# A convolution and gated MLP on one core: the convolution's steps in a new order, its transfers on two queues by name

## The chip, the cores and the metric

The kernel runs on one core of a Trainium2 chip. The core has five engines that run side by side, each in the order of its own instructions: TensorE (PE, with its weight loads shown as PEld), VectorE (DVE), ScalarE (ACT), GpSimd (POOL) and SyncE (SP). Transfers are issued by SP, POOL or ScalarE and carried out by 16 DMA engines. The metric is the device time of one execution in microseconds; less is better. Where the text says clock, it is the share of TensorE's full clock that the profile shows as granted.

## The reference

Two residual blocks on a sequence of 2048 tokens with 576 channels, both modulated by a vector `c`:

```python
mod = (_silu(c) @ w_mod).reshape(c.shape[0], 6, 1, -1)
h = _layernorm(x) * (1 + ca) + sa
x = x + ga * A(h)          # a long convolution, with u * Dskip
h = _layernorm(x) * (1 + cb) + sb
x = x + gb * B(h)          # a gated MLP that mixes tokens
```

`A` builds for each of 576 channels a kernel of length 2048 from 128 complex poles, `K[d, l] = Re(sum_n C P^l dB)` with `P = exp(dt * A)`, and convolves it with the sequence (in the reference by an FFT of length 4096). `B` is `z = gelu(h @ w_in)`, split in `z1` and a layer-normed `z2` (2304 columns each), `g = w_sp @ z2 + b_sp` over the 2048 tokens, and `(z1 * g) @ w_out`.

## The kernel before

The program has three parts one after the other: the convolution (`ssm`), the first half of the MLP (`phase_a`: layer norm, `z2`, and the splitting of weights into two halves of 16 bit) and its second half (`phase_b`: token mixing, gate and output). The change is in the first alone, up to the point where the first block of tokens is transposed for `phase_a`.

The convolution is written as some 50 kinds of small steps, functions under the decorator `step`, and a list, `ORDER` (line 172), of 1172 words such as `u_p.1.3`: a kind and its indices. A loop goes through the list and calls one function per word. The instructions are kept in program order on each engine, so the list fixes what each engine does after what; between engines the program waits by semaphores. An engine whose next instruction lacks its data stands still, also where later ones could run; the same holds for a queue of transfers.

The steps, in the order in which data goes through them:

- `pole_in`, `pl.0.k`, `pl.1.k`, `pload`: load the poles (set 0 is the first quarter, set 1 the rest), prepare phases and logarithms in 24 small stages on VectorE and ScalarE, store them split in three 16-bit parts, load them back in another layout.
- `load`, `mod_init`, `m_l`, `m_p`, `m_a`, `m_q`, `m_e`: constants and the modulation vectors.
- `x_l`, `st_a`, `st_v`, `ln_r`, `ln_p`, `ln_a`: the layer norm of 16 token blocks, its transform on TensorE, and the store of the result to memory (`u1_d`). `turn` ends this: all of `u1_d` is stored, and its buffers are given to the convolution.
- For each of 36 groups of 16 channels: `e_p`, `e_a` (exponentials), `t_p`, `t_i`, `t_b`, `s_f`, `s_c` (phases rounded to a period, sines), `p_a`, `p_b`, `p_c` (their products on VectorE), `kg_p`, `kg_a`, `kg_d` (the kernel, with Dskip), `k1_p`, `k1_e` (its transform). `MODE` gives for each group how the phase is rounded: 0 with a ScalarE pass and two VectorE passes; 1 to 4 with the rounding done by additional matmuls (12 instead of 4), and then a VectorE copy and a VectorE pass (1), one VectorE pass (2), a ScalarE copy and a VectorE pass (3) or one ScalarE pass (4). `COPY` says whether `k1_e` runs on VectorE ("1") or ScalarE ("0").
- For each of five channel blocks `c` (four of 128 channels, one of 64) and its parts `i`: `u_l` (load from `u1_d`), `u_p`, `u_a` (with two transfers that swap the halves of a tile), `z_p`, `z_m` (multiply with the kernel's transform), `v_p`, `v_a` (with the store to `v_d`).
- For each block and quarter `q`: `y_v` (load of `v_d`, once all its parts are stored), `y_x` (load of the residual), `y_p`, `y_s` (add, and store to `x1_d`).
- `wpre`, `ml.*`: steps of the MLP taken into the list: the loads of `w_in` for `z2` (`start_load`), their sums, scales and splitting, the first token block's layer norm. `end` gives back the memory of the tables; `ml.start` (line 1104) sets up the MLP's tiles in it and loads `ident`, `mrow`, `x1l` and `xz`, four transfers on SP.

Queues: the function `Q` puts a load on POOL's queue where its word stands in `GPQ` (line 167), else on SP's. Only loads go through `Q`. The stores of `ln_a`, `v_a` and `y_s`, the swaps of `u_a` and the loads of `pload` are on POOL; `st4_l`, `wpre`, `ml.start`, `ml.start_x1` and `ml.start_load` are on SP.

Of the kernel before, what the change touches and what calls it, by code (L numbers as in the profile page):

```python
# [18 lines left out]
D = 576  # L19
# [8 lines left out]
CHL = CHW[-1]  # L28
# [161 lines left out]
k1_p.5 kg_a.6 t_p.9 k1_e.5 u_l.0.5 kg_d.6 t_i.9 s_c.8 u_l.0.3 k1_e.4 t_p.10 t_i.10 t_b.9 s_f.9 t_b.10 s_c.9 kg_p.7 p_a.8 p_b.8 kg_a.7 kg_d.7 u_p.0.0  # L190
p_c.8 s_f.10 u_p.0.1 k1_p.6 k1_e.6 u_a.0.0 e_p.9.0 e_a.9.0 k1_p.7 e_p.11.0 u_a.0.1 kg_p.8 kg_a.8 e_a.11.0 k1_e.7 p_a.9 u_p.0.5 p_b.9 p_c.9 kg_d.8
e_p.10.0 e_a.10.0 u_p.0.3 t_p.11 u_a.0.3 t_i.11 cst_l.0 t_p.12 pload.2.0 t_i.12 z_p.0.0 s_c.10 t_b.12 u_a.0.5 u_l.0.4 kg_p.9 s_c.12 z_m.0.0 u_l.2.2
kg_a.9 s_f.12 t_b.11 s_c.11 pload.2.2 s_f.11 y_x.0.2 kg_d.9 p_a.10 z_p.0.1 z_m.0.1 p_b.10 p_c.10 v_p.0.0 u_l.1.3 k1_p.8 k1_e.8 v_a.0.0 u_p.0.2 p_a.11
cst_l.3 p_b.11 e_p.15.1 e_p.15.0 e_a.15.1 e_a.15.0 cst_l.1 t_p.14 e_p.12.1 t_i.14 e_a.12.1 u_l.1.0 z_p.0.3 kg_p.10 u_a.0.2 e_p.14.0 kg_a.10 kg_d.10
e_a.14.0 t_b.14 z_m.0.3 v_p.0.1 v_a.0.1 e_p.12.0 e_a.12.0 p_a.12 e_p.14.1 e_a.14.1 e_p.13.1 e_a.13.1 e_p.13.0 st4_l p_b.12 e_a.13.0 k1_p.10 k1_e.10
p_c.11 z_p.0.2 k1_p.9 s_c.14 u_p.0.4 u_a.0.4 t_p.13 s_f.14 t_i.13 k1_e.9 u_l.0.7 v_p.0.3 u_l.1.2 t_p.15 p_c.12 kg_p.12 v_a.0.3 t_b.13 z_m.0.2 t_i.15
p_a.14 t_b.15 kg_a.12 s_f.13 kg_d.12 kg_p.11 kg_a.11 p_b.14 p_c.14 s_c.15 v_p.0.2 t_p.16 s_f.15 z_p.0.5 z_m.0.5 v_a.0.2 s_c.13 p_a.13 p_b.13 pload.2.1
k1_p.12 t_i.16 t_b.16 s_c.16 s_f.16 kg_d.11 kg_p.14 kg_a.14 kg_d.14 u_p.1.0 u_l.1.1 u_a.1.0 u_p.1.3 u_a.1.3 p_c.13 z_p.0.4 z_m.0.4 k1_e.12 e_p.18.1
k1_p.14 k1_e.14 e_p.16.0 e_a.16.0 e_a.18.1 kg_p.13 e_p.17.1 t_p.17 p_a.15 kg_a.13 p_b.15 p_c.15 kg_d.13 e_p.17.0 e_a.17.0 u_p.0.7 t_i.17 u_l.0.6
u_p.0.6 u_a.0.6 e_p.18.0 k1_p.11 u_a.0.7 e_a.18.0 t_b.17 u_l.1.7 k1_p.13 k1_e.13 k1_e.11 e_p.16.1 e_a.16.1 t_p.18 e_a.17.1 t_i.18 t_b.18 s_c.17  # L200
v_p.0.5 v_a.0.5 u_l.1.4 p_a.16 p_b.16 s_c.18 p_c.16 s_f.18 s_f.17 v_p.0.4 v_a.0.4 e_p.19.0 e_a.19.0 z_p.0.6 z_m.0.6 kg_p.15 kg_a.15 e_p.20.0 kg_p.16
v_p.0.6 v_a.0.6 e_a.20.0 e_p.19.1 e_a.19.1 e_p.21.1 e_a.21.1 p_a.18 t_p.20 t_i.20 p_b.18 kg_d.15 k1_p.15 pload.3.0 z_p.0.7 e_p.20.1 t_b.20 kg_a.16
p_c.18 k1_e.15 z_m.0.7 y_x.0.0 e_a.20.1 t_p.19 z_p.1.0 z_m.1.0 t_i.19 u_p.1.2 u_p.1.7 u_p.1.1 kg_d.16 t_b.19 p_a.17 s_f.20 u_a.1.2 s_c.20 p_b.17
p_c.17 s_c.19 kg_p.18 kg_a.18 kg_d.18 v_p.1.0 v_a.1.0 s_f.19 pload.3.1 t_p.21 t_i.21 u_a.1.1 p_a.20 p_b.20 v_p.0.7 v_a.0.7 e_p.21.0 e_a.21.0 z_p.1.3
z_m.1.3 e_p.22.0 u_a.1.7 k1_p.16 k1_e.16 wpre.0 kg_p.17 kg_a.17 e_p.23.1 p_c.20 k1_p.18 kg_d.17 e_a.22.0 e_a.23.1 z_p.1.1 e_p.22.1 t_p.22 k1_e.18
p_a.19 p_b.19 k1_p.17 e_a.22.1 t_i.22 t_b.21 z_m.1.1 e_p.23.0 e_a.23.0 p_c.19 t_b.22 s_c.21 u_l.1.6 kg_p.20 z_p.1.2 kg_a.20 t_p.23 t_i.23 t_b.23
s_f.21 v_p.1.3 v_a.1.3 s_f.23 s_c.23 k1_e.17 kg_p.19 kg_a.19 u_p.1.6 u_a.1.6 z_m.1.2 kg_d.20 k1_p.20 k1_e.20 u_p.1.4 u_a.1.4 p_a.21 p_b.21 p_c.21
kg_d.19 p_a.23 p_b.23 t_p.24 t_i.24 t_b.24 v_p.1.2 v_a.1.2 kg_p.21 s_f.22 k1_p.19 k1_e.19 u_l.2.3 kg_a.21 kg_d.21 s_c.22 s_c.24 pload.3.2 p_a.22
p_b.22 e_p.27.0 v_p.1.1 v_a.1.1 u_p.2.3 u_a.2.3 k1_p.21 s_f.24 y_v.0.0 z_p.1.7 k1_e.21 p_c.22 z_m.1.7 y_p.0.0 e_p.27.1 e_a.27.1 wpre.1 p_c.23 e_p.24.0
e_a.24.0 y_s.0.0 kg_p.22 kg_a.22 kg_d.22 e_p.24.1 z_p.1.4 e_a.27.0 z_m.1.4 u_l.2.0 t_p.26 t_i.26 e_a.24.1 t_b.26 kg_p.23 kg_a.23 y_v.0.1 kg_d.23  # L210
e_p.26.0 e_a.26.0 v_p.1.4 e_p.25.0 e_p.25.1 e_a.25.1 u_l.1.5 u_p.1.5 v_a.1.4 p_a.24 p_b.24 p_c.24 e_a.25.0 u_a.1.5 u_l.2.6 k1_p.23 k1_e.23 t_p.27
k1_p.22 t_i.27 t_b.27 y_x.0.1 e_p.28.0 e_a.28.0 y_p.0.1 y_s.0.1 e_p.26.1 e_a.26.1 k1_e.22 z_p.1.6 t_p.25 t_i.25 z_p.1.5 s_c.26 u_p.2.2 z_m.1.5 t_b.25
t_p.30 kg_p.24 kg_a.24 s_f.26 u_l.2.4 p_a.26 u_a.2.2 p_b.26 v_p.1.7 v_a.1.7 v_p.1.5 s_f.25 v_a.1.5 e_p.32.0 p_c.26 s_c.25 y_v.0.2 z_m.1.6 u_p.2.0
u_a.2.0 s_c.27 p_a.25 y_p.0.2 y_s.0.2 u_p.2.4 u_l.2.1 u_l.2.5 kg_p.26 s_f.27 kg_a.26 y_x.1.3 z_p.2.2 z_m.2.2 kg_d.26 p_b.25 e_a.32.0 p_c.25 v_p.1.6
v_a.1.6 t_i.30 u_a.2.4 z_p.2.0 z_m.2.0 k1_p.26 t_b.30 k1_e.26 t_p.28 y_v.0.3 t_i.28 v_p.2.2 kg_d.24 e_p.28.1 e_a.28.1 u_p.2.1 v_a.2.2 u_a.2.1 e_p.30.1
# [23 lines left out]
def ssm(tc, I, x1_d, consts_s, dram, mod_d, mlp):  # L239
    nc = mlp.tied  # L240
# [4 lines left out]
    with ExitStack() as ctx:  # L245
# [174 lines left out]
        def pload(c, n):  # L420
# [5 lines left out]
            for h in range(2):  # L426
                G.dma_start(t_[64 * h:64 * h + 48], d_[c, h, k:k + 6].rearrange("q (c g n) -> (q c) g n", c=8, g=9))
# [1933 lines left out]
```

## Time and profile before

| what | us |
|---|---|
| time, median of 3 runs | 1761.44 (1759.05 to 1761.78) |
| the profiled execution's own time | 1761.1 |
| its span in the profile | 1759.3 |
| busy in the span: PE, DVE, ACT, POOL | 1661.2, 1253.8, 832.4, 275.0 |
| the first transpose of `phase_a` (the list's end) | at 428.05 |
| the first matmul of `phase_b` | 682.74 |

The profile shows one execution; times in it count from its start. An engine's busy time is the union of its instructions' spans; the ends of matmuls are modelled, so a busy PE need not be PE at its peak. In rows of the timeline stand start, duration, engine, line, operation, what it writes and reads, the number of instructions merged, and in brackets the idle time of the engine before the first of them and what ended it. Nearly all rows name line 152, that of the helper which records the instructions; tiles tell them apart: `u<-u_d` is `u_l`, `u<-v_d` is `y_v`, `pk<-u,small` is `u_p`, `pk<-small,kab` is `k1_p`, `pk<-u,st` is `y_p`, `u_d<-st1o` the store of `ln_a`, `wst` the weights of `start_load`, `pg<-et,ft` is `p_a` or `p_b`.

### The profile page before, as it was taken

What the parts mean: (1) busy time and instruction counts of PE and PEld (TensorE: products, weight loads), DVE (VectorE), ACT (ScalarE), POOL (GpSimd) and SP (SyncE); (2) the same over time, 40 slices, a digit from 0 to 9 for tenths busy, and PEclk for the clock granted to TensorE, in tenths of its full rate; (3) what the DMA queues carried; (4) which work ended last, traced back from release to release, by engine and by line L of the source; (5) the groups of instructions that cost most, each with busy time, mean ns of one, the idle gap of its engine ahead of it and who ended that gap; (6) DMA issues with size and microseconds to landing.
All of it is one profiled execution on the core that took longest, in us unless ns stands there. A gap on an engine that the chain in (4) does not pass through costs nothing. (4 is left out here: it accounts for less than half of the span.)

```text
span 1759.3 us, 36489 instructions
## 1 busy us (share of the span) xinstructions
PE 1661.2 (94%) x15246; PEld 1240.5 (71%) x15246; DVE 1253.8 (71%) x2254; ACT 832.4 (47%) x1107; POOL 275.0 (16%) x442
## 2 busy tenths in 40 slices
PE   4687999987999999999999999999999999999999
PEld 1244666655455445778878888888888888888887
DVE  5887888857989996788998777787343487334432
ACT  4868999853676664455443443333222223122210
POOL 3343334333122210000000000000111100111100
PEclk9678999998999999999999999999999999999999
DMA  8566656788598888677665877674766563556531
GB/s 237 175 194 204 182 153 185 209 234 270 187 297 259 236 246 270 246 258 280 213 203 184 315 266 269 233 241 138 243 228 233 190 217 104 204 201 208 192 109 42
DMA packets 167061, 376.25 MB, mean 214 GB/s; under 512 B 36288, under 2 KB 85056, under 8 KB 166128
## 3 DMA queue, kind: packets, MB, share of 16 engines
q0 software_dynamic: 40176, 183.48, 31.6%
q1 hardware_dynamic: 120816, 163.77, 30.7%
q10 hardware_dynamic: 5904, 26.67, 3.7%
q8 instruction: 120, 1.97, 0.5%
q14 instruction: 45, 0.37, 0.1%
HBM read 263.11 MB, written 101.31 MB: 207 GB/s over the span
## 5 line engine op out<-in xcount | busy, mean ns | idle before, releaser
L152 PEld LDWEIGHTS <-zset 128*128 128x128 f16 x7182 | 701.8, 98 | 93.5 <-DVE zset L152 8.5
L152 PE MATMUL ps<-wsp,zset 128*128 128x256 f16 x6048 | 667.7, 273 | 8.0 <-DVE zset L152 6.5
L152 PE MATMUL pz<-wz,nt 128*128 128x512 f16 (+1 forms) x1120 | 222.1, 358 | 10.8 <-DVE nt L152 4.3
L152 ACT ACTIVATE z<-gt 128x1024 f16<-128x1024 f32 x56 | 59.0, 1054 | 289.4 <-DVE gt L152 289.4
L152 PEld LDWEIGHTS <-nt 128*128 128x128 f16 x1120 | 109.0, 98 | 117.7 <-DVE nt L152 5.7
L2069 POOL DMA_DIRECT2D zset<-set_d x96 | 50.8, 529 | 870.0 <-PE ps L152 627.8
L152 DVE SCALAR_TENSOR_TENSOR gt<-ps,sc,bsp 128x512 f32<-128x512 f32 x36 | 27.0, 750 | 205.2 <-PE ps L152 203.4
L152 PE MATMUL ps<-wout,z 128*128 128x288 f16 x1344 | 170.0, 286 | 0.0
L152 PEld LDWEIGHTS <-z 128*128 128x128 f16 x1344 | 131.5, 98 | 33.0
L152 PE MATMUL ps<-n2o,zset 128*128 128x256 f16 x1134 | 128.2, 273 | 0.0
L152 DVE TENSOR_TENSOR raw<-raw 128x512 f32<-128x512 f32 (+2 forms) x228 | 119.1, 528 | 12.3 <-DMA raw<-z_d 7.8
L152 DVE SCALAR_TENSOR_TENSOR gt<-ps,sc,gt 128x512 f32<-128x512 f32 (+1 forms) x180 | 122.2, 696 | 7.6
L152 DVE TENSOR_TENSOR zset<-raw,zset 128x1792 f16<-128x1792 f32 x48 | 96.9, 2019 | 16.2 <-ACT zset L152 16.1
L152 ACT ACTIVATE zset<-raw 128x1792 f16<-128x1792 f32 x48 | 81.0, 1691 | 56.7 <-PE ps L152 20.6
L152 DVE TENSOR_TENSOR z<-ps,z 128x512 f32<-128x512 f32 (+1 forms) x126 | 71.9, 598 | 36.8 <-ACT z L152 25.0
L152 DVE TENSOR_TENSOR pg<-et,ft 128x1024 f32<-128x1024 f32 x72 | 85.5, 1218 | 3.3 <-PE pk L152 2.0
L152 PE MATMUL pk<-zz,small 128*128 128x512 f32 x144 | 70.1, 613 | 0.0
L152 ACT ACTIVATE wsp<-raw,sc 128x1792 f16<-128x1792 f32 x25 | 44.6, 1785 | 42.7 <-DVE raw L152 35.0
L152 ACT ACTIVATE z<-z,sc 128x1024 f32<-128x1024 f32 x21 | 24.1, 1148 | 75.6 <-DVE z L152 71.9
L152 DVE TENSOR_TENSOR zz<-pk,uu 128x1024 f32<-128x1024 f32 x36 | 44.0, 1221 | 19.8 <-PE pk L152 18.9
L152 ACT ACTIVATE z<-pz,sc 128x512 f32<-128x512 f32 (+1 forms) x96 | 51.5, 582 | 13.5 <-DMA z_d<-z 11.8
L152 ACT ACTIVATE z<-z,nm,r 128x1152 f32<-128x1152 f32 x24 | 31.5, 1342 | 54.1 <-DVE nm L152 31.6
(311 smaller groups left out, 2409.0 us busy)
## 6 DMA issues: line engine op xcount, KB each, us to landing
zset<-set_d POOLq DMA_DIRECT2D x96, 896.0 KB, 5.0
raw<-z_d SPq DMA_DIRECT2D x48, 512.0 KB, 5.7
set_d<-zset ACTq DMA_DIRECT2D x24, 896.0 KB, 6.1
z_d<-z POOLq DMA_DIRECT2D x32, 576.0 KB, 9.6
zset<-wa_d POOLq DMA_DIRECT2D x18, 896.0 KB, 4.9
raw<-in_w_spT SPq DMA_DIRECT2D x25, 512.0 KB, 4.4
set_d<-zset SPq DMA_DIRECT2D x12, 896.0 KB, 5.8
u_d<-st1o POOLq DMA_DIRECT2D x16, 576.0 KB, 3.8
```

What stands on the lines that cost most here:

```text
L152: return self.tc.keep_in_program_order(f(*a, **k))
L2069: self.nc.gpsimd.dma_start(o, self.set_d[f, j - 1] if j else self.wa_d[f])
```

## The change

- `ORDER` is another list of the same steps, with three new ones. `MODE`, `COPY` and `GPQ` are set anew with it. `MODE` has 16, 2, 6, 4 and 8 groups of modes 0 to 4 where it had 17, 3, 6, 6 and 4. `COPY` puts 22 of 36 copies on VectorE where it put 14. `GPQ` names 123 steps where it named 41.
- The stores of `ln_a`, `v_a` and `y_s`, the swaps of `u_a`, the loads of `pload`, `st4_l`, `wpre`, `start_load` and `start_x1` go through `Q` too: on SP's queue unless their word stands in `GPQ`.
- The loads of `mrow`, `x1l` and `xz` leave `ml.start` and become the steps `ml.ld_m`, `ml.ld_l` and `ml.ld_z`, placed in the list by themselves.

By the lists, SP issues 122 transfers before and 177 after, POOL 258 (memsets included) and 203.

The parts of the list that the text speaks of, before:

```
... ln_p.14.1 s_c.7 e_p.10.1 p_a.7 p_b.7 ln_a.14.1 e_a.11.1 ln_p.14.0 ln_a.14.0 turn u_l.0.2 cst_l.2 kg_p.6 p_c.7
... z_p.3.7 kg_p.34 kg_a.34 kg_d.34 k1_p.35 k1_e.35 k1_e.33 k1_p.34 end ml.start ml.ap y_x.4.1 u_p.4.1 y_x.4.0
    u_a.4.1 k1_e.34 u_p.3.4 z_m.3.7 y_v.1.2 ml.start_sum.1 v_p.3.1 v_a.3.1 z_p.3.5 u_a.3.4 v_p.3.7 v_a.3.7 z_m.3.5
    y_p.1.2 ml.start_x1 ml.win_scale.6.0
... y_s.3.1 y_s.4.1 y_v.3.2 y_p.3.2 y_s.3.2 y_v.4.2 y_p.4.2 y_x.4.2 y_s.4.2 y_v.4.3 ml.start_load.3 y_p.4.3 y_s.3.3 y_s.4.3
```

and after:

```
... ln_p.14.0 ln_a.14.0 e_p.8.1 e_a.8.1 e_p.9.1 e_a.9.1 ln_p.14.1 ln_a.14.1 turn t_p.8 t_i.8 cst_l.2 p_a.7 p_b.7 p_c.7
    e_p.8.0 e_a.8.0 p_a.6 p_b.6 p_c.6
... z_p.3.0 k1_p.35 k1_e.35 y_v.1.2 z_m.3.0 kg_d.33 y_p.1.2 kg_p.34 kg_a.34 u_a.4.2 k1_p.33 kg_d.34 k1_p.34 end
    ml.start ml.ld_z ml.start_sum.1 ml.start_load.2 ml.ld_l k1_e.33 v_p.3.0 v_a.3.0 u_p.4.0 y_s.1.2
... y_s.4.1 y_x.4.3 y_p.4.2 y_s.4.2 y_p.3.2 y_x.3.3 y_p.4.3 y_s.4.3 y_x.3.1 y_s.3.1 y_x.3.2 y_s.3.2 ml.start_load.3 y_s.3.3
```

The rest of the diff, cut to its core:

```diff
-MODE = [int(k) for k in "333301130222221440204304000000000000"]
-COPY = "010001110000011111010000000100100011"
+MODE = [int(k) for k in "332433110422204440022444000000000000"]
+COPY = "110011111110011111111100010001100100"
...
         def pload(c, n):
+            Q_ = Q("pload", c, n)
...
-                G.dma_start(t_[64 * h:64 * h + 48], d_[c, h, k:k + 6].rearrange("q (c g n) -> (q c) g n", c=8, g=9))
+                Q_.dma_start(t_[64 * h:64 * h + 48], d_[c, h, k:k + 6].rearrange("q (c g n) -> (q c) g n", c=8, g=9))
...
-            G.dma_start(u1_d[:, b:b + 2, :, :, c].rearrange("g b r k d -> (b r k) g d"), o)
+            Q("ln_a", b, h).dma_start(u1_d[:, b:b + 2, :, :, c].rearrange("g b r k d -> (b r k) g d"), o)
...
         def wpre(q):
             mlp.nc = nc
+            mlp.ldq = Q("wpre", q)
             mlp.start_load(q, pools["wpre"])
...
-            G.dma_start(uu[:64, 1], uu[64:, 0])
-            G.dma_start(uu[64:, 1], uu[:64, 0])
+            Q("u_a", c, i).dma_start(uu[:64, 1], uu[64:, 0])
+            Q("u_a", c, i).dma_start(uu[64:, 1], uu[:64, 0])
...
-            G.dma_start(v_d[c][:, kr(c, i)], by(v, c))
+            Q("v_a", c, i).dma_start(v_d[c][:, kr(c, i)], by(v, c))
...
-            G.dma_start(x1_d[bs, :, chan(c)].rearrange("b p d -> p b d"), xb)
+            Q("y_s", c, q).dma_start(x1_d[bs, :, chan(c)].rearrange("b p d -> p b d"), xb)
...
         def ml(name, *a):
-            mlp.nc = nc
+            mlp.nc, mlp.ldq = nc, Q("ml", name, *a)
...
     def win_load(self, t, c0, n):
-        S, I = self.nc.sync, self.I
+        S, I = self.ldq or self.nc.sync, self.I
...
-        S.dma_start(mrow, self.mod_d[:2].partition_broadcast(128))
...
-        S.dma_start(self.x1l, I["x"][:, 4:, D - CHL:])
...
-        S.dma_start(self.x1f[:, :, 384:], I["x"][:, :4, 384:])
         self.stg = self.pool(self.c2, "stg", 2)
 
+    def ld_m(self):
+        self.ldq.dma_start(self.mrow, self.mod_d[:2].partition_broadcast(128))
+
+    def ld_l(self):
+        self.ldq.dma_start(self.x1l, self.I["x"][:, 4:, D - CHL:])
+
+    def ld_z(self):
+        self.ldq.dma_start(self.x1f[:, :, 384:], self.I["x"][:, :4, 384:])
+
     def start_x1(self):
-        self.nc.sync.dma_start(self.x1f[:, :, :384], self.x1_d[:4, :, :384].rearrange("b p d -> p b d"))
+        self.ldq.dma_start(self.x1f[:, :, :384], self.x1_d[:4, :, :384].rearrange("b p d -> p b d"))
```

More of the change, by code (lines that the diff above doesn't have):

```diff
@@ L190 @@
[L190 to L193, printed above, removed]
@@ L206 @@
[L206 to L209, printed above, removed]
@@ L210 @@
[L210 to L213, printed above, removed]
@@ L226 @@
-p_a.35 e_p.34.0 u_p.4.2 t_b.34 e_p.34.1 u_a.3.7 u_a.4.2 p_b.35 p_c.35 e_a.34.0 e_a.34.1 y_x.2.1 u_l.4.3 v_p.3.3 v_a.3.3 kg_p.33 kg_a.33 kg_d.33
-y_p.2.0 k1_p.32 z_p.3.1 y_s.2.0 z_m.3.1 s_c.34 k1_e.32 u_l.3.5 s_f.34 p_a.34 v_p.3.0 v_a.3.0 u_l.3.4 u_p.3.5 u_a.3.5 kg_p.35 k1_p.33 y_v.2.3 p_b.34
-p_c.34 kg_a.35 kg_d.35 z_p.3.7 kg_p.34 kg_a.34 kg_d.34 k1_p.35 k1_e.35 k1_e.33 k1_p.34 end ml.start ml.ap y_x.4.1 u_p.4.1 y_x.4.0 u_a.4.1 k1_e.34
-u_p.3.4 z_m.3.7 y_v.1.2 ml.start_sum.1 v_p.3.1 v_a.3.1 z_p.3.5 u_a.3.4 v_p.3.7 v_a.3.7 z_m.3.5 y_p.1.2 ml.start_x1 ml.win_scale.6.0 v_p.3.5 v_a.3.5
```

126 lines of the change are left out of this document (73 added, 53 removed).

## The prediction

> **What bounds the kernel now.** I read the page first, then busy time by stretches, the timeline at the places where TensorE idles, the waits of the DMA queue, and the groups of instructions for durations. The page's span and engine totals, and the stretches that I cut at the changes of regime (columns: stretch, length, busy us and instructions of PE, PEld, DVE, ACT, POOL, then granted TensorE clock, DMA share, GB/s):
>
> ```profile
> span 1759.3 us, 36489 instructions
> ...
> PE 1661.2 (94%) x15246; PEld 1240.5 (71%) x15246; DVE 1253.8 (71%) x2254; ACT 832.4 (47%) x1107; POOL 275.0 (16%) x442
> ```
>
> ```profile
> 0.00:60.00 60.00, 27.36 (x121) 9.64 (x122) 40.35 (x119) 35.45 (x64) 22.30 (x40) 0.94 0.75 206
> 60.00:160.00 100.00, 73.63 (x1189) 39.97 (x1188) 83.56 (x176) 78.11 (x108) 32.58 (x49) 0.72 0.62 197
> 160.00:365.00 205.00, 204.91 (x2967) 124.58 (x2966) 178.33 (x218) 183.92 (x245) 82.33 (x136) 1.00 0.65 187
> 365.00:430.00 65.00, 50.52 (x433) 35.77 (x430) 37.00 (x91) 23.78 (x30) 25.55 (x38) 0.87 0.88 263
> 430.00:685.00 255.00, 242.29 (x1280) 125.36 (x1279) 230.55 (x692) 168.72 (x259) 51.88 (x68) 1.00 0.82 248
> ```
>
> The changed list is the convolution alone, the first 428 us; what follows keeps its code and starts when the list ends, so a microsecond won before 428 is one won at the end. Of those 428 us, 205 are TensorE without a gap: no order of steps makes them shorter, except by moving TensorE's work out of them. What an order can win lies before 160 us (no engine above 84%), where the layer norm hands over to the convolution, and after 365, where transfers set the pace (0.88 of the DMA engines).
>
> The hand-over, on POOL, SP, PE and DVE:
>
> ```profile
> 146.74 0.75 POOL L152 DMA_DIRECT2D u_d<-st1o  x1 [2.31 <-ACT st1o L152]
> ...
> 150.85 0.77 POOL L152 DMA_DIRECT2D u<-u_d  x1 [2.82 <-DVE k L152]
> ```
>
> ```profile
> 150.33 1.63 SPq L152 DMA_DIRECT2D u<-u_d  x3
> ```
>
> ```profile
> 151.83 0.29 PE L152 MATMUL pk<-et,pg 128*32 128x64 f32 x8
> 156.97 3.75 PE L152 MATMUL pk<-u,small 128*128 128x512 f32 x4 [4.84 <-DMA u<-u_d]
> 160.65 1.62 PE L152 MATMUL pk<-small,kab 128*64 128x128 f32 x16
> ```
>
> ```profile
> 162.32 0.69 DVE L152 COPY k<-pk 128x512 f32<-128x512 f32 x1 [4.01 <-PE pk L152]
> ```
>
> ```profile
> 152.00:157.00 5.00, 0.16 (x11) 0.07 (x1) 4.71 (x6) 4.92 (x7) 0.57 (x1) 0.79 0.97 281
> 157.00:162.00 5.00, 5.00 (x20) 2.46 (x20) 1.31 (x3) 1.88 (x2) 1.08 (x2) 0.52 0.47 135
> ```
>
> The last store of the layer norm (`ln_a.14.0`) is issued at 146.7, the first loads (`u_l`) at 150.3 when it has landed, and TensorE gets their data at 157.0. It has run out of other work at 152.1, waits 4.84 us, and then runs at a granted clock of 0.52.
>
> The tail: SP's queue (first its longest wait on VectorE between 160 and 430 us, then its issues), then PE and DVE:
>
> ```profile
> SPq L152 <- DVE kab L152: 12.4, 1, 12.4
> ```
>
> ```profile
> 367.98 0.33 SPq L152 DMA_DIRECT2D mrow<-mod_d  x1
> 368.36 0.44 SPq L152 DMA_DIRECT2D x1l<-in_x  x1
> 368.89 1.12 SPq L152 DMA_DIRECT2D xz<-in_x  x1
> 370.29 4.61 SPq L152 DMA_DIRECT2D u<-v_d  x1
> ```
>
> ```profile
> 381.83 0.66 PE L152 MATMUL pk<-u,st 128*64 128x128 f32 x2 [6.39 <-DMA u<-v_d]
> ```
>
> ```profile
> 385.48 0.16 DVE L152 COPY sc<-pk 128x1 f32<-128x1 f32 x1 [10.49 <-PE pk L152]
> ```
>
> `ml.start` puts the load of `mrow` on SP; its memory is that of the tables, so it waits 12.4 us for the last `kg_d`. Behind it stand `x1l`, `xz` and the loads of `y_v.1.2`, whose first takes 4.61 us to issue, and TensorE, whose next step is `y_p.1.2`, stands still for 6.39 us, VectorE for 10.49.
>
> **The change part by part.** *Engines.* Durations of what `MODE` and `COPY` move:
>
> ```profile
> L152 ACT ACT_TABLE_LOAD x37 | 47.5, 1283 | 1.4 <-PEq L2350 0.7
> ...
> L152 DVE SCALAR_TENSOR_TENSOR ft<-ft,ps 128x1024 f32<-128x1024 f32 x17 | 20.6, 1213 | 2.2 <-ACT ft L152 2.2
> ...
> L152 ACT ACTIVATE ft<-ps 128x1024 f32<-128x1024 f32 x20 | 20.6, 1029 | 2.1 <-PE ps L152 2.1
> ...
> L152 DVE TENSOR_SCALAR ft<-ft 128x1024 int32<-128x1024 int32 x26 | 18.1, 701 | 3.4 <-ACT ft L152 2.8
> ...
> L152 ACT ACTIVATE k<-pk 128x512 f32<-128x512 f32 x22 | 13.2, 602 | 1.0 <-PE pk L152 0.8
> ```
>
> Modes 0 to 4 go from 17, 3, 6, 6, 4 groups to 16, 2, 6, 4, 8. On VectorE mode 0 costs 1.21 + 0.70 us, mode 1 about the same, mode 3 0.70, mode 4 nothing: 1.9 + 1.9 + 2 x 0.7 = 5.2 us less. Eight more `k1_e` copies go to VectorE, at about the 0.69 of the copy quoted above: 5.5 us more. VectorE ends even, at +0.3. ScalarE loses the eight copies (-4.8) and gains two passes of about 1.03 net and loses one of like size (+1): 3.8 us less. TensorE gets one more group with the rounding matmuls (eight more, 0 to 1.6 us at 0.2 each; I take 0.6). These sums are small because the plan rebalances; the rest is order.
>
> *Start, 0 to 150 us.* Counting where the list goes from exponentials to sines and back reproduces the 37 table loads of the page; the new list has 36, but 12 instead of 15 before `turn`: 3 x 1.28 = 3.8 us less of ScalarE there. It idles 21.9 us between 60 and 160, so most of this may be covered; without that cover it is worth the 3.8. The first steps are also exchanged:
>
> ```profile
> 11.43 0.17 DVE L152 TENSOR_SCALAR ec<-ec 96x6 f32<-96x6 f32 x1 [5.16 <-ACT ec L152]
> ...
> 13.15 0.67 ACT L152 ACTIVATE st1o<-ln_x 128x576 f32<-128x576 f32 x1
> ```
>
> `mod_init`, behind which VectorE's pole steps queued for 5.16 us, comes far later; but `st_a.0.0`, whose VectorE part needs `x_l.0` (here at 13.15), comes far earlier, so VectorE, with some 4 us of work listed ahead of it, waits there instead: about 5 us. I put the whole stage at -1. Bounds: all table loads and the removed wait without a substitute, -9; the new wait with one further statistics step behind it, +3.
>
> *Hand-over.* In the new list `p_a` to `p_c` of groups 6 and 7 stand behind `turn` instead of mostly before:
>
> ```profile
> L152 DVE TENSOR_TENSOR pg<-et,ft 128x1024 f32<-128x1024 f32 x72 | 85.5, 1218 | 3.3 <-PE pk L152 2.0 <-ACT ft L152 1.0
> ...
> L152 DVE SCALAR_TENSOR_TENSOR et<-ft,et 128x512 f32<-128x512 f32 x36 | 24.8, 689 | 0.8
> ```
>
> That is 2 x (2 x 1.22 + 2 x 0.69) = 7.6 us of VectorE's work which now lies in the 10.2 us between the last store (146.74) and the data (156.97), so the stores can go out earlier by up to as much, and there is work while they fly. Won: the 4.84 us gap and what the low clock cost behind it, by these rows at full clock:
>
> ```profile
> 257.58 1.02 PE L152 MATMUL pk<-u,small 128*128 128x512 f32 x2
> ...
> 258.53 0.85 PEld L152 LDWEIGHTS pk<-small,kab 128*64 128x64 f32 x16 [0.76 <-issue]
> 258.54 1.09 PE L152 MATMUL pk<-small,kab 128*64 128x128 f32 x16
> ```
>
> 3.75 - 2 x 1.02 = 1.7 and 1.62 - 1.09 = 0.5, together with the gap 7.0 at most. VectorE's own gap says 4.0 at least if the data come in time. I take -6, with 0 as the other bound, should the loads still be late.
>
> *Middle.* TensorE-bound before, and I see nothing that ends that: through the middle VectorE's listed work leads TensorE's by the same in both lists (by 23.8 us before and 24.6 after at `p_c.20`, 21.8 and 20.4 at `p_c.35`, adding up the list with mean durations like those quoted). `k1_p.7` (1.0), `e_p.9.0` and `e_p.11.0` (some 0.3 each) move ahead of the first `u_p`, so 1.6 less is left there; with the 0.6 above, -1. What it may cost is the first rival.
>
> *Tail.* `y_v.1.2` now stands before `end` on SP and the loads of `mrow`, `x1l`, `xz` (`ml.ld_*`) on POOL's queue behind it, so the 6.39 us end; late next is whatever the DMA engines deliver last. They were busy 0.88 of 65 us, or 57 us, and the bytes are nearly the same, so at most 7.8 us can go. I take two thirds of that, -5; bounds -7.8 and 0.
>
> *End of the list.* A loss:
>
> ```profile
> 428.05 0.76 PE L152 MATMUL pt<-ident,n 128*128 128x128 f32 x5
> ```
>
> ```profile
> 424.05 10.11 SPq L152 DMA_DIRECT2D wst<-in_w_in  x6
> ```
>
> ```profile
> 434.01 2.34 ACT L152 ACTIVATE wz<-wst 128x2560 f16<-128x2560 f32 x1 [4.34 <-DMA wst<-in_w_in]
> ```
>
> ```profile
> uu<-in_x SPq DMA_DIRECT2D x4, 256.0 KB, 4.4
> ```
>
> Before, `ml.start_load.3` is issued 4 us ahead of the first transpose of the next phase. Now the stores `y_s.4.3`, `y_s.3.1` and `y_s.3.2` stand ahead of it on SP; `y_s.3.1` needs `y_x.3.1`, a load that stands on POOL behind `y_s.4.2` and `y_x.3.3`: two issues of 0.75 and 4.4 to landing, about 6 us after `y_s.4.2`. So the weights come later by about 5, against 1 or 2 of slack. Bounds: 0 (the DMA engines are free by then) and +6; I take +5.
>
> The sum: -1 - 6 - 1 - 5 + 5 = -8, against the profiled execution's own 1761.1 (span 1759.3 and 1.8 around it): **1753**. The median of the runs shown is 1761.44, 0.3 above it, so the same holds there.
>
> **The rivals.** *Stores before loads (slower).* SP issued only what waits for free buffers; it now issues results of ScalarE and VectorE too (155 transfers up to `end` by the list, 88 before). In a queue that goes in order, each `u_l` or `y_v` behind an `u_a` or `v_a` store waits for that result. For it: the 12.4 us above are just such a block. Against it: POOL's queue mixed both kinds all along, and the middle had no TensorE wait on a transfer. A late `u_l` costs what it cost at 152, 4.84 + 2.2 = 7.0. It decides from the second one on: two give 1753 + 14 = 1767.
>
> *Transfers are the bound (no change).* The tail's 5 are not won, since its transfers only queue up elsewhere: -3, so 1758. For it: the share of 0.88. Against it: the 5 us after 152 and the 12.4 us wait were ordering, not bandwidth. The Trainium skill speaks for this rival: its page "DMA: Bandwidth & Descriptors", section "Issuing engines are not separate DMA queues", says that transfers share the same 16 engines whoever starts them, and that a second issuer saves only the time to issue. By that rule the second queue adds nothing in the tail; the 6.39 us here were a place in a queue, which the rule leaves open.
>
> *The start gains too (much faster).* VectorE idles 19.7 + 16.4 = 36 us up to 160; if the new order takes a quarter of that, 9 us, beyond the sum, it is 1744. For it: no engine is a bound there. Against: each idle piece is short, and every exchange adds its own.
>
> That the change does not do what it says (steps out of the listed order) I give nothing: tables and queue order before agree with the list.
>
> **How the numbers follow.** Forecast 0.45 (its own range 1748 to 1757), start too 0.15, transfers 0.18, stores before loads 0.22. A measurement of this kernel tells 0.2%, 3.5 us, from no change. Faster: the first two, 0.60; the same: 0.18; slower: 0.22. Range 1743 to 1766: it holds the forecast, the start's gain, the transfers' case and the lighter half of the last rival.
>
> **What would show it.** Hand-over: no TensorE wait on `u<-u_d` over 1 us and no half-clock stretch around 150. Tail: no wait of several us on `u<-v_d` by `y_p.1.2`, and the first transpose 9 to 14 us before 428. End: the weights (`wst`) landing about 11 us after that transpose instead of 6. The forecast is wrong if PE has gaps between 160 and 360 that end on a transfer (slower), or if the first `u_p` comes at 157 as before.

## The result, and the profile after

The changed kernel takes 1745.05 us in the median of 4 runs (1741.92 to 1747.86), against 1760.96 (1759.05 to 1761.78) for the kernel before in the same series: a ratio of 0.9911, 95% interval 0.9887 to 0.9934, or 12 to 20 us less. A later series gave 0.9921 (0.9905 to 0.9936). The forecast was 1753. Single executions of one and the same kernel spread by up to 15 us, so what follows compares ratios to the kernel before, run on the same chip, and takes 15 us (the mean of 0.9911 and 0.9921) for the gain. The profiled execution is the shortest of the four: 1741.92, span 1740.2, 19.1 us below the span before.

The page's span and totals, and busy time by the stretches used for the kernel before:

```profile
span 1740.2 us, 36526 instructions
...
PE 1644.8 (95%) x15254; PEld 1241.0 (71%) x15254; DVE 1254.4 (72%) x2256; ACT 826.4 (47%) x1099; POOL 246.3 (14%) x387
```

```profile
0.00:60.00 60.00, 26.23 (x169) 10.97 (x170) 41.56 (x119) 35.93 (x66) 23.04 (x40) 0.92 0.75 203
60.00:160.00 100.00, 80.45 (x1302) 45.10 (x1300) 91.12 (x186) 83.01 (x113) 29.03 (x45) 0.77 0.75 223
160.00:365.00 205.00, 200.15 (x2991) 131.39 (x2989) 177.91 (x228) 181.18 (x241) 59.01 (x88) 1.00 0.71 203
365.00:430.00 65.00, 46.10 (x317) 28.40 (x317) 44.08 (x118) 22.71 (x30) 23.96 (x35) 0.84 0.70 212
430.00:685.00 255.00, 246.19 (x1351) 132.36 (x1350) 227.41 (x657) 167.71 (x255) 50.62 (x65) 1.00 0.83 258
```

From 60 to 160 us VectorE is busy 91.1 instead of 83.6 and TensorE 80.5 instead of 73.6. From 160 to 365 TensorE, without a gap before, is now busy 4.8 us less. To put the gain in its places I count the listed TensorE steps that have started by a time, each with the duration it had before in the full stretch (u_p 0.96, v_p 1.82, z_p 0.99, kg_p and k1_p 1.03), and subtract that work from the clock. What remains is the time without listed work:

| by | before | after | change since the line above |
|---|---|---|---|
| 150 us | 48.3 | 42.0 | -6.3 (start) |
| 160 us | 54.3 | 41.6 | -6.4 (hand-over) |
| 365 us | 55.9 | 37.9 | -5.3 (middle) |
| first transpose (428.05; 403.34) | 74.6 | 49.3 | -7.3 (tail) |
| from there to the first matmul of `phase_b` | 254.7 | 262.1 | +7.4 (end of the list) |

These are one execution of each kernel. In a second trace of the changed kernel (last experiment), counted the same way, the stages come to about -4, -6, -5, -8 and, from 405.38 to 664.39, +4.3: single stages scatter by 2 or 3 us.

With 0.6 us of added work the first transpose comes 24.7 us earlier, the first matmul of `phase_b` 17.3 (665.42 for 682.74), and the span ends 19.1 earlier.

The hand-over, and the one wait of TensorE on a transfer in the middle (timeline, PE):

```profile
148.19 2.84 PE L152 MATMUL pk<-u,small 128*128 128x512 f32 x6
...
224.00 1.10 PE L152 MATMUL pk<-u,small 128*128 128x512 f32 x2 [1.54 <-DMA u<-u_d]
```

The first three `u_p` stand in a row at 148.2, without a wait ahead of them and at 0.95 us each: the 4.84 us gap and the half clock are gone. (The granted clock is 1.00 from 145 to 160 us; a stretch at 0.69 now lies ahead of that, from 140 to 145.) All of TensorE's waits from 160 to 365 us (us in total, times, longest), where before there were none:

```profile
PE pk L152 <- issue: 1.6, 2, 0.9
PE pk L152 <- DMA u<-u_d: 1.5, 1, 1.5
PE pk L152 <- DVE zz L152: 1.1, 3, 0.7
PE pk L152 <- DVE sc L152: 0.2, 1, 0.2
```

The end of the list; first PE before, then PE, SP's queue and ScalarE after:

```profile
433.18 1.47 PE L152 MATMUL pz<-wz,nt 128*128 128x512 f16 x6 [1.72 <-DVE nt L152]
436.49 0.38 PE L152 MATMUL pz<-acc,ones 128*128 128x1 f32 x2 [1.85 <-ACT wz L152]
```

```profile
403.34 0.77 PE L152 MATMUL pt<-ident,n 128*128 128x128 f32 x5
...
413.36 2.74 PE L152 MATMUL pz<-wz,nt 128*128 128x512 f16 x6 [6.66 <-DVE nt L152]
418.95 0.38 PE L152 MATMUL pz<-acc,ones 128*128 128x1 f32 x2 [2.86 <-ACT wz L152]
```

```profile
406.77 1.77 SPq L152 DMA_DIRECT2D x_d<-uu  x2
408.60 5.74 SPq L152 DMA_DIRECT2D wst<-in_w_in  x6
```

```profile
416.47 2.34 ACT L152 ACTIVATE wz<-wst 128x2560 f16<-128x2560 f32 x1 [11.56 <-DMA wst<-in_w_in]
```

`ml.start_load.3` is issued at 408.6, behind the stores of `y_s.3.1` and `y_s.3.2`; its weights are there at 416.47, 13.1 us behind the first transpose, where before it was 434.01 - 428.05 = 6.0. The forecast said about 11. The two waits of TensorE shown here grow by 6.66 + 2.86 - 1.72 - 1.85 = 6.0 us; in the second trace of the changed kernel (6.45 and 2.38) by 5.3.

### The profile page after: what moved, and what is told of

Its sections match the earlier page's. It is cut to its first block, busy times and chain, and to the rows that moved or that the text cites. A ratio compares the mean times of both kernels' runs of the same rounds, so it can differ in the third digit from the quotient of the medians.

```text
span 1740.2 us, 36526 instructions
## 1 busy us (share of the span) xinstructions
PE 1644.8 (95%) x15254; PEld 1241.0 (71%) x15254; DVE 1254.4 (72%) x2256; ACT 826.4 (47%) x1099; POOL 246.3 (14%) x387
## 4 chain that ended last, share of the span: by engine, by line
PE 64%; DVE 17%; issue 4%; DMA 4%; ACT 3%; POOL 1%; SPq 0%; ACTq 0%; DVEq 0%; POOLq 0%
PE ps L152 57%; PE pk L152 8%; DVE bsz L152 2%; DVE n L152 2%; DVE zset L152 1%; DVE gt L152 1%; DVE rq L152 1%; DMA v_d<-v 1%; DVE pg L152 1%; ACT ft L152 1%; DVE wso L152 1%; DVE wsp L152 1%; DMA wst<-in_w_in 1%; DVE nt L152 1%; DVE raw L152 1%
## 5 line engine op out<-in xcount | busy, mean ns | idle before, releaser
L152 DVE TENSOR_TENSOR zset<-raw,zset 128x1792 f16<-128x1792 f32 x48 | 96.9, 2020 | 14.6 <-ACT zset L152 14.6
L152 ACT ACTIVATE z<-z,nm,r 128x1152 f32<-128x1152 f32 x24 | 31.5, 1342 | 52.4 <-DVE nm L152 30.9
L152 PE MATMUL ps<-n2q,wf 128*128 128x512 f16 x252 | 55.7, 379 | 0.0
```

The lines of the kernel that those rows point to most:

```text
L152: return self.tc.keep_in_program_order(f(*a, **k))
```

## The experiments

### One list, two halves

Two lists are put together from both, cut where the two have done nearly the same steps (just behind the hand-over). Each half keeps its own modes, copies and queues.

```diff
 h1_oldstart
-ORDER = new[0:]
+ORDER = old[:334] + [w for w in new if w not in old[:334]]
 h2_newstart
-ORDER = new[0:]
+ORDER = new[:328] + [w for w in old if w not in new[:328]]   # ml.ld_* behind ml.start
```

> A list of both: the first 334 words (past turn, to e_a.10.1) in the order before, with the modes, copies and queues of before for them; all later words in the changed order, with its modes, copies and queues. From TensorE's time without listed work the profiled gain of 24.7 us at the first transpose is 6.3 (to 150 us) + 6.4 (hand-over) + 5.3 (160 to 365) + 7.3 (tail) less 0.6 of added work, and 7.4 is lost behind it. Theory 'stages add': this keeps only the last three, 5.3 + 7.3 - 7.4 = 5 less than before: 1756. Rival 'the later stages take it back' (the middle or the tail is paced by something that does not depend on when it starts, such as the transfers): as the changed kernel, 1745 to 1748.

> The reverse: the first 328 words (to t_b.8) of the changed list with its modes, copies and queues, all later words in the order before with the modes, copies and queues of before (the three loads taken out of ml.start stand right behind it). Theory 'stages add': 6.3 + 6.4 = 12.7 less than before: 1748, first transpose at 415.4. The forecast as it was put gave these stages 1 + 6 = 7: 1754. Rival 'the tail takes it back' (transfers pace the end, which the old order leaves as it was): 1756 to 1761.

Measured: the old start with the new rest 0.9955 (0.9939 to 0.9972), 7.9 us less than before; the new start with the old rest 0.9962 (0.9948 to 0.9976), 6.7 less. By its interval each is good to 2 or 3 us. The two add up to the 15 of the whole: the stages add, and the halves are about equal. Neither half is what the table of one execution says (12.7 for the new start, 5.2 for the rest); counted the same way, the new start's own trace here is only some 6 us ahead by 160 us. By `u_p.0.0` the six traces taken of the new start lie at 147.3 to 152.5, the five of the old one at 154.6 to 161.3, 8 us apart in the mean, and by 160 us the new start is some 11 us ahead in the mean. So start and hand-over are worth 7 by the times, as forecast (1 + 6), and perhaps more by the traces; the rest is worth 8 by the times, where 1 was forecast.

### What TensorE pays for a change of form

In both traces the same step takes different times, and it depends on its neighbours: a `u_p` 0.86, 0.95, 0.96 or 1.06 us from its start to the next one's, as none, the one behind, the one ahead or both of them differ from it in the form of their weights. (Forms: `u_p`, `v_p`, `z_p`, `e_p.*.1` use weights of 128 x 128; `e_p.*.0` and `t_p` two halves of rows; `k1_p` and `y_p` two halves of 64 columns; `kg_p` four parts of 32.) Counted by these forms, the list before changes 169 times between 160 and 365 us, the new one 92 times. First the cost by itself:

```diff
+        for f, g in ((pA, pC), (pA, pK), (pA, pR)):
+            for p_ in (f, g) * 8:      # in turn
+                p_()
+            for _ in range(8): f()     # then in groups
+            for _ in range(8): g()
         for word in ORDER:
```

> The changed kernel with a probe ahead of its list, on constant data, results unused, so that its time is no measure: steps like u_p (A: weights 128 x 128), like k1_p (C: two halves of 64 columns), like kg_p (K: four parts of 32 columns) and like e_p.*.0 (R: two halves of 48 rows), first eight times in turn (A C A C ...), then eight A and eight C; the same with A and K, A and R. Theory 'passes': TensorE pays at each change of the weights' form, about 0.14 us (between 0.10 and 0.19): the alternating 16 steps take 14 x 0.14 = 2 us longer than the grouped 16 for each of the three pairs, whatever else the kernel does. Rival 'order' (the durations differ because of what else runs then): no difference, under 0.3 us.

The probe's timeline on PE, pair A and R: first in turn, then grouped (the last row is the next step's):

```profile
73.31 1.13 PE L152 MATMUL pk<-pg 128*128 128x512 f32 x2
74.37 0.39 PE L152 MATMUL ps<-pg 48*128 48x512 bf16 x2
74.69 1.12 PE L152 MATMUL pk<-pg 128*128 128x512 f32 x2
...
82.96 7.13 PE L152 MATMUL pk<-pg 128*128 128x512 f32 x16
90.03 1.90 PE L152 MATMUL ps<-pg 48*128 48x512 bf16 x16
91.86 2.13 PE L152 MATMUL ps<-wm,ec 96*32 96x288 f32 x24
```

In turn, A and R take 74.69 - 73.31 = 1.38 us a pair; eight of each grouped take 8.90, 1.11 a pair. The steps, by their starts:

| step like | in turn | in a group | dearer by |
|---|---|---|---|
| u_p (A), beside any of the others | 1.056 | 0.858 | 0.198 |
| k1_p (C) | 1.024 | 0.873 | 0.151 |
| kg_p (K) | 1.031 | 0.893 | 0.138 |
| e_p.*.0 (R) | 0.319 | 0.216 | 0.103 |

A pair has two changes, so one change costs (0.198 + 0.103) / 2 = 0.15 to (0.198 + 0.151) / 2 = 0.17 us. It does not matter what runs beside it: from 8 to 20 us, where A and C stand in turn, ScalarE is busy 9.55 of the 12 us and the DMA share is 1.03; from 73.31 to 82.96, where A and R do, VectorE, ScalarE and POOL are busy 0.00 and the share is 0.01; A takes 1.056 to 1.059 in both. As whole sequences A and R take 11.02 us in turn and 8.90 in groups, the 2 us expected; A and C take 18.6 and 14.2, a difference in which 1.9 is the surplus of the first three steps, slow at the program's start (2.00, 1.91 and 1.15); A and K are longer in groups, 19.3 against 16.7, for waits of another kind that are told in the last section. The rival, that the durations differ because of what else runs, falls. The Trainium skill's page "TensorEngine Tiling (Array Packing)", section "Key Properties", says that changing the tiling mode, not just the tile, drains TensorE. The trace agrees that such a change costs time, 0.15 to 0.17 us; that it is a drain, and that these forms are the page's modes, no run here shows.

Then the changed kernel with its runs broken up, and the kernel before with runs made:

```diff
 e1_pe_mixed (39 exchanges of neighbours like this one)
-... v_p.0.2 u_l.1.7 z_m.0.6 k1_p.15 k1_e.15 ...
+... k1_p.15 v_p.0.2 u_l.1.7 z_m.0.6 k1_e.15 ...
 e2_before_runs (24 like this one)
-... kg_p.17 kg_a.17 e_p.23.1 p_c.20 k1_p.18 kg_d.17 ...
+... kg_p.17 kg_a.17 k1_p.18 e_p.23.1 p_c.20 kg_d.17 ...
```

> The changed kernel, in which 39 pairs of neighbouring TensorE steps between u_p.0.0 and k1_p.35 are exchanged; all else as it is. In the two traces a u_p, v_p or z_p takes about 0.10 us more where the TensorE step before it is not of its family (u_p, v_p, z_p, e_p.*.1), and about 0.09 more where the one after it is not. The list before passes between the family and the rest 162 times, the changed one 78 times, this one 156 times. Theory 'passes' (the stretch 160 to 365 us won 5.3 us because TensorE passes less often): 78 passes x 0.095 = 7.4 us later, the first transpose of the next phase at 410 to 411 instead of 403.3, and the time 1752 against 1745. Rival 'order' (the stretch won because steps and transfers stand in better places; the passes are an artefact of the modelled ends of matmuls): an exchange of neighbours moves nothing by more than 2 us, so 1745 +- 1.5 and the transpose at 403 to 404.

> The kernel before, in which 24 pairs of neighbouring TensorE steps in the same stretch are exchanged so that passes fall from 162 to 114; lists of modes, copies and queues as before. Theory 'passes': 48 x 0.095 = 4.6 us less in the stretch that TensorE fills; the first transpose at 423.5 instead of 428.05, time 1756.5 against 1761. If the tail is paced by transfers alone, 2 of these are lost again there: 1758.5. Rival 'order': no change, 1761 +- 1.5.

The first came out as 'passes' said: 0.9961 (0.9947 to 0.9976), 7.9 us slower than the changed kernel where 7.4 was worked out; in the profiled execution the first transpose is at 415.6, later than the 410 to 411 expected, with 2.4 us of the surplus in new waits. The second did not: 1.0030 (1.0018 to 1.0043), 5.3 us slower than before. What TensorE waited for in it from 160 to 365 us (us in total, times, longest):

```profile
PE ps L152 <- DVE ft L152: 3.6, 3, 1.2
PE pk L152 <- DVE et L152: 1.3, 1, 1.3
PE ps L152 <- ACT ft L152: 1.3, 2, 0.9
PE pk L152 <- DVE xb L152: 1.0, 2, 0.5
```

The kernel before has not one such wait. Split by steps, the 205 us are (shortest: each step with the shortest time that it has anywhere; forms: what its steps took beyond that):

| kernel | changes of form | shortest | forms | waits |
|---|---|---|---|---|
| before | 169 | 180.9 | 23.4 | 0.1 |
| changed | 92 | 185.7 | 14.6 | 4.9 |
| changed, mixed (e1) | 151 | 176.6 | 21.6 | 7.3 |
| before, runs (e2) | 135 | 176.5 | 19.8 | 8.7 |
| before, fewer runs (below) | 152 | 183.4 | 20.4 | 1.3 |

The forms follow their count in every row, 0.13 to 0.16 us for each change. In e1 they grew by 7.0 us against the changed kernel, and waits by 2.4. In e2 they fell by 3.6 us, and 8.6 of waits came in. The likely reason, not shown: TensorE and VectorE (178 of the 205 us) were so closely fitted in the old list that a neighbour's place, some 1 or 2 us, leaves TensorE without data. To see whether the runs pay where no wait follows, ten exchanges were taken back:

```diff
 e9_before_runs2: e2 without the exchanges of
-z_p.0.0/kg_p.9  v_p.0.1/e_p.12.0  v_p.0.2/t_p.16  e_p.19.0/z_p.0.6  k1_p.21/z_p.1.7
-v_p.1.4/e_p.25.0  u_p.2.4/kg_p.26  v_p.2.3/k1_p.27  u_p.3.3/kg_p.29  v_p.2.6/e_p.35.0
```

> The kernel before with 14 of the 24 exchanges of the earlier version, leaving out those behind which TensorE waited there; passes 162 to 134. Theory 'passes, and waits took them back': 28 x 0.095 = 2.7 us less in 160 to 365 us, few waits left: 2 to 3 us faster than before. Rival 'any exchange costs': TensorE's waits come up elsewhere, no change or slower.

In its trace the stretch does 2.5 us more work than before (last row, and in its time without work from 160 to 360 us: -1.1 against +1.4), as expected; in the time nothing is left, 0.9998 (0.9985 to 1.0010). Inconclusive: 2.7 is at the edge of what the interval holds. So added changes were shown to cost time; that fewer of them alone make the old list faster was not.

### The start: are the table loads covered?

```diff
+        def x_s():
+            A.activation(dum, halfpi, AF.Sin)
-... e_a.1.1 ... e_a.3.1 ... e_a.5.1 ... e_a.10.1 ...
+... e_a.1.1 x_s ... e_a.3.1 x_s ... e_a.5.1 x_s ... e_a.10.1 x_s ...
```

> The changed kernel with four sines of one column placed between exponentials ahead of turn (behind e_a.1.1, e_a.3.1, e_a.5.1, e_a.10.1): eight more table loads of 1.28 us, some 11 us more of ScalarE before 140 us. Theory 'covered' (the forecast put the three table loads less, 3.8 us, at nearly nothing, since ScalarE idles): no more than 3 us slower than the changed kernel. Rival 'table loads set the start': all 11 show, 1753 to 1756 on a scale where before is 1758 and the changed kernel 1743.

Groups of ScalarE, changed kernel, then this one:

```profile
L152 ACT ACT_TABLE_LOAD x36 | 46.2, 1283 | 2.8 <-DVE sc L152 1.4 <-PEq L2362 0.8
```

```profile
L152 ACT ACT_TABLE_LOAD x44 | 56.5, 1283 | 3.2 <-DVE sc L152 1.7 <-PEq L2385 0.8
```

Eight loads more, 56.5 - 46.2 = 10.3 us, and 0.9964 (0.9949 to 0.9979): 7.6 us slower than the changed kernel in the same series (0.9921). In its trace the loss is there before the convolution's first `u_p`, which comes at 157.24 us (148.19 and 150.37 in the two traces of the changed kernel). 'Covered' falls: a table load added before `turn` shows with about three quarters of its time (7.6 of 10.3, with some 4 us of uncertainty on the 7.6), although ScalarE is busy only 83.0 of the 100 us from 60 to 160. If the three loads less weighed the same, they were worth about 2.8 us; those three were not tried by themselves.

### The queues

```diff
 e5_stores_pool: GPQ
-(the words of ln_a, v_a, y_s, u_a, pload named there only in part; ml.ld_l ml.ld_m ml.ld_z)
+(all words of ln_a, v_a, y_s, u_a, pload; none of ml.*, wpre, st4_l)
```

> The changed kernel with the queues by the rule before: the stores of ln_a, v_a, y_s, the swaps of u_a and the loads of pload all on POOL, st4_l, wpre and the MLP's loads all on SP; the list, its modes and copies, and the queues of all other loads as changed. Theory 'order' (the gains come from the places of steps; which of two queues issues a store matters little, as long as no load stands behind a late one): 13 to 17 us less than before, as the changed kernel, with no new TensorE wait over 1 us in 160 to 365 us. Rival 'two queues' (spreading the stores is what lets the order work, as POOL takes about 0.75 us for an issue and SP 0.35): the stores back up on POOL, the swaps of u_a come late, TensorE waits on zz or u several times, 5 us or more of the gain are lost: at most 11 less than before.

Measured: 1.0223 (1.0206 to 1.0239), 39 us slower than before and 54 slower than the changed kernel. Both theories fall short; the rival had the direction and not the size. The stretch from 160 to 365 us, a `u_p` that waits, and POOL's queue ahead of it:

```profile
160.00:365.00 205.00, 182.99 (x2765) 117.17 (x2764) 163.36 (x202) 169.26 (x221) 76.22 (x125) 0.93 0.59 172
```

```profile
178.30 2.05 PE L152 MATMUL pk<-u,small 128*128 128x512 f32 x2 [7.62 <-DMA u<-u_d]
```

```profile
173.00 0.55 POOL L152 DMA_DIRECT2D uu<-uu  x1 [11.66 <-ACT uu L152]
174.14 0.54 POOL L152 DMA_DIRECT2D uu<-uu  x1 [0.59 <-issue]
174.67 0.79 POOL L152 DMA_DIRECT2D u<-u_d  x1
```

The load of `u_l` stands on POOL behind the swap of a `u_a` whose copy on ScalarE is late; POOL stands still for 11.66 us, TensorE for 7.62 and its `u_p` then takes 2.05 us, twice the usual. This is the rival "stores before loads", with 7 us as its price for each late load, on the other queue. Three such waits take 17.7 us in the middle. A longer one comes at the start, on one of the loads of `pload`, which was on SP at 34.92 us in the changed kernel:

```profile
58.46 0.93 PE L152 MATMUL ps<-sel,la 48*128 48x256 bf16 x2 [13.35 <-DMA la<-pa_d]
```

```profile
48.50 3.75 POOL L152 DMA_DIRECT2D pb_d<-pt  x6 [8.69 <-DVE pt L152]
52.24 3.70 POOL L152 DMA_DIRECT2D pa_d<-pt  x6
55.93 1.03 POOL L152 DMA_DIRECT2D la<-pa_d  x2
```

Here it stands on POOL behind twelve stores of the poles, and TensorE waits 13.35 us. Together that is 31 of the 54 us; how the rest divides was not worked out. The transfers themselves are less busy from 160 to 365 us, 0.59 against 0.71: what counts is what stands behind what, not how much one queue can carry.

### The tail and the end of the list

```diff
 e7_before_yv (kernel before)
-end ml.start ml.ap y_x.4.1 u_p.4.1 y_x.4.0 u_a.4.1 k1_e.34 u_p.3.4 z_m.3.7 y_v.1.2 ...
+end y_v.1.2 ml.start ml.ap y_x.4.1 u_p.4.1 y_x.4.0 u_a.4.1 k1_e.34 u_p.3.4 z_m.3.7 ...
 e6a_load3, e6b_load3_yx (changed kernel)
-y_v.4.3 ... y_x.3.3 y_p.4.3 y_s.4.3 y_x.3.1 y_s.3.1 y_x.3.2 y_s.3.2 ml.start_load.3 y_s.3.3
+y_v.4.3 ml.start_load.3 ... y_x.3.3 y_p.4.3 y_s.4.3 y_x.3.1 y_s.3.1 y_x.3.2 y_s.3.2 y_s.3.3
+y_v.4.3 y_x.3.3 y_x.3.1 y_x.3.2 ml.start_load.3 ... y_p.4.3 y_s.4.3 y_s.3.1 y_s.3.2 y_s.3.3
```

> The kernel before with one step moved: y_v.1.2 ahead of ml.start, so on SP its loads stand ahead of that of mrow, which waits 12.4 us for memory. Theory 'place in the queue': TensorE's wait of 6.39 us on u<-v_d at y_p.1.2 goes; what is late next costs 1 or 2: 5 us less than before, first transpose at 423. Rival 'transfers pace the tail' (busy 0.88 of 65 us): the wait only moves to later y_v, the first transpose stays at 427 to 428 and the time within 1 of before.

> The changed kernel with one step moved: ml.start_load.3 stands behind y_v.4.3 instead of behind y_s.3.2, so on SP it is no longer behind three stores of results. Theory 'the end' (the 7.4 us lost behind the first transpose are the late weights: landed 13.1 us after the transpose against 6.0 before): the weights land 7 us earlier, ScalarE's pass on them too; TensorE's wait of 2.86 us on it goes, that of 6.66 on VectorE, which stands behind the late loads y_x.3.1 and y_x.3.2, stays: 3 us less than the changed kernel, 19 less than before. Rival 'transfers': the load takes bandwidth from y_v.3.2 and y_v.4.3, whose y_p come later by as much: no change.

> The changed kernel with ml.start_load.3 and also the three loads y_x.3.1, y_x.3.2, y_x.3.3 placed behind y_v.4.3, ahead of all the last stores on both queues. Theory 'the end': both waits behind the first transpose (6.66 and 2.86) mostly go: 7 us less than the changed kernel, 23 less than before; first matmul of phase_b 254 to 256 us behind the first transpose (262.1 in the changed kernel, 254.7 before). Rival 'transfers': four loads of 256 KB and more collide with y_v.3.2 and y_v.4.3, TensorE waits for those instead (some 4 us): 2 to 3 less than the changed kernel at best.

The first took TensorE's wait at `y_p.1.2` from 6.39 us to 0.68, and the time by 2.3 us, if at all: 0.9987 (0.9970 to 1.0003), an interval that holds both theories, 5 us less and no change. The trace, of this kernel's longest execution (1763.4), says more. Its step as TensorE sees it, and the stretch from where 309 us of listed work are done to the first transpose, for before, for this kernel and for the changed one:

```profile
380.69 1.09 PE L152 MATMUL pk<-u,st 128*64 128x128 f32 x14 [0.68 <-DMA u<-v_d]
```

```profile
365.00:428.00 63.00, 49.27 (x426) 35.03 (x422) 35.29 (x88) 23.02 (x28) 23.55 (x36) 0.86 0.88 260
```

```profile
369.60:430.80 61.20, 52.26 (x422) 37.07 (x421) 34.64 (x87) 23.04 (x28) 23.15 (x35) 0.83 0.92 268
```

```profile
347.00:403.30 56.30, 47.35 (x432) 33.57 (x428) 33.91 (x85) 24.00 (x30) 33.35 (x48) 0.91 0.87 263
```

With the last column these are 63.0 x 260 = 16.4 MB, 61.2 x 268 = 16.4 MB and 56.3 x 263 = 14.8 MB. Taking the wait away leaves the bytes, and the stretch shrinks by 1.8 us only: TensorE's waits in it fall from 13.7 to 8.8 us in all, but its granted clock from 0.86 to 0.83. The changed kernel has 1.6 MB less in its stretch, worth 6 us at 263 GB/s, of the 6.7 us by which it is shorter. (The middle carries more: 203 GB/s where it was 187. And the last weights have slipped behind the end.) So 'transfers' holds for the tail in part; how far, the last of the three shows.

The load of the weights alone moved brought nothing: 0.9925 (0.9910 to 0.9941); TensorE's 2.86 us on ScalarE went, its wait on VectorE grew from 6.66 to 8.3:

```profile
PE pz L152 <- DVE nt L152: 8.3, 1, 8.3
```

With the three `y_x` as well it is 0.9902 (0.9888 to 0.9916), 1739.47 to 1740.75 in four runs. Its PE, ScalarE, and the stretch to its first transpose:

```profile
405.63 0.76 PE L152 MATMUL pt<-ident,n 128*128 128x128 f32 x5
...
413.43 2.54 PE L152 MATMUL pz<-wz,nt 128*128 128x512 f16 x6 [4.45 <-DVE nt L152]
```

```profile
407.08 2.34 ACT L152 ACTIVATE wz<-wst 128x2560 f16<-128x2560 f32 x1
```

```profile
346.00:405.60 59.60, 46.33 (x432) 32.72 (x428) 34.19 (x85) 23.99 (x30) 33.75 (x48) 0.91 0.91 278
```

ScalarE's pass on the weights waits for nothing, the wait on VectorE is 4.45, and the first matmul of `phase_b` comes 257.6 us behind the first transpose (663.2 - 405.6) instead of 262.1 and, in the second trace of the changed kernel, 259.0. But from the first `u_p` (147.28) to that transpose it is 258.4 us, some 3 more than in either of the two (255.2 and 255.0), since the four loads are now among the tail's transfers, 59.6 us at 278 GB/s, or 16.6 MB. Of the 7 us expected some 2 to 3 remain by the ratios, as 'transfers' said.

This also weighs the bytes: 1.8 MB put back cost the tail 3.3 us (59.6 for 56.3), where 263 GB/s would give 6.7, and with as many bytes as before it is still 3.4 us shorter than before (63.0). So about half of the tail's gain is bytes that left it. The rest has no cause shown; the removed wait (1.8 in its own trace) can be part of it. So can the packets: the 16.6 MB go in 10233 of them, before in 18645. That was not tried.

### The changed kernel once more

> The changed kernel once more, unaltered, for comparison with the others of this series and with the version that has the last loads placed earlier (0.9902 of before). From its first ratio, 0.9911: 15 to 16 us less than before, single executions from 1740 to 1748. If the list's start is what scatters, the first step ln_p.2.1 lies at 50 us in short executions and at 53 to 54 in long ones.

It gave 0.9921 (0.9905 to 0.9936), 1742.02 to 1746.56, and in its trace `ln_p.2.1` stands at 52.4, in an execution of 1742.13, between the two places expected: by this one trace the start scatters, but does not part the long from the short. The version with the loads moved is 0.0019, 3 us, faster by its ratio; the intervals overlap, but each of its four runs is below each of the nine of the changed kernel (1741.92 the lowest). Its ratio is the lowest measured.

## Why the prediction was right, and where not

The time lies in the range, and the direction and the place of half of the gain are as forecast; the gain is 15 us where 8 were forecast.

- **The premise on the middle failed**: "no order of steps makes them shorter". TensorE had no gap in the 205 us, but part of its busy time was paid for changes of form, and an order can save those: 23.4 us before, 14.6 after. Net of 4.9 of new waits the middle won 5.3 in the traces, not 1. The forecast gave every kind of step one price, and no rival in it would have moved the middle's work itself; the rule cited above from the Trainium skill ("TensorEngine Tiling (Array Packing)", "Key Properties") might have suggested one. That a change of form costs time is shown by the probe and by the list with its runs broken up; that the 77 changes fewer are the whole gain of the middle is worked out from the split, and the old list with fewer changes was not faster.
- **Start, -1**: too small by the traces (6.3 in the first, about 4 in the second by 150 us). The cover named for the three table loads was not there; at three quarters they would be worth 2.8. Start and hand-over together are 7 in the halves, as summed; how much of it is the start's stays open, as they can't be parted cleanly, since the products of groups 6 and 7 went from the one to the other.
- **Hand-over, -6**: right, gap and half clock gone, 6.4 in the trace.
- **Tail, -5**: about the size (7.3), in large part by another cause. The forecast put it all on the removed wait on SP, with "the bytes are nearly the same". By itself the removed wait was worth 2.3 us (about 5 at most by its interval), and 1.6 of 16.4 MB left the tail, where 1.8 MB put back cost 3.3; the rest is open. The forecast had the rival "transfers are the bound". The Trainium skill ("DMA: Bandwidth & Descriptors", "Issuing engines are not separate DMA queues") spoke for it; the trace agrees so far as the stretch holds 16.4 MB whether or not the wait is there, and is 1.8 us shorter without it.
- **End of the list, +5**: right, for the reason given: 7.4 in the first trace and 4.3 in the second, 6.0 and 5.3 in the two waits. Moving the loads back took half of those waits away (4.45 left of 9.52), but brought 2 to 3 us of time at most, so a part of the end's loss is the tail's own gain deferred. Tail and end together are 0 in the forecast, 0.1 in the first trace and some -3 to -4 in the second.
- **Rivals**: "stores before loads" did not come: one wait of 1.54 us on `u<-u_d` in the middle. The mechanism is real, as the other assignment of queues shows, and its price near (7.62 us of waiting and about 1 of slow work for the one shown, 7.0 forecast); this list, with these queues, keeps late results out of the way. The longest wait there, 13.35 us for a load of `pload` at the start, is not among what the forecast feared. "The start gains too" has the time (1744) nearest to the measured one, but not the place.

## What to carry to other kernels

An engine that is busy without a gap can still be shortened by order, if one and the same step shows two durations: sort a step's durations by its neighbours before taking a mean. A list and its queues are one plan: neighbours exchanged or a queue reassigned without planning anew cost 5 and 54 us here. Before crediting a removed wait, multiply the stretch's rate by its length: where the bytes stay, much of the wait can come back elsewhere. The mean rate prices bytes too high, though: 1.8 MB would be 6.7 us by it, and cost 3.3 when they were put back.

## What the hardware showed that was not expected

The price of a change of form, 0.15 to 0.17 us, is nearly the same for the three pairs tried (within 0.03 us). And steps of many small matmuls, eight `kg_p` in a row of 64 instructions each, stop about every second step for a cause that the profile does not name:

```profile
63.54 1.99 PE L152 MATMUL pk<-pg 128*32 128x64 f32 x128 [1.40 <-issue]
67.00 1.99 PE L152 MATMUL pk<-pg 128*32 128x64 f32 x128 [1.46 <-issue]
70.45 2.61 PE L152 MATMUL pk<-pg 128*32 128x64 f32 x99 [1.46 <-issue]
```

Alternating with long matmuls they do not. So grouping has a limit: for `kg_p` a second one in a row saves 0.3 us of changes, and the changed kernel's 1.6 us of 'issue' in the middle may be of this kind. The cause was not tried.
